# A new order for all steps of an attention and feed-forward kernel, with one pool of single PSUM banks and five output row buffers

## The chip, the cores and the metric

The kernel runs on one core of a Trainium2 chip. The metric is the device time of one execution in microseconds; of several runs the median counts. The engines are TensorE (PE, with its weight loads as PEld), VectorE (DVE), ScalarE (ACT), GpSimd (POOL) and SyncE (SP). Each works through its own queue in order and waits for the others by semaphores.

## The reference, cut to what matters

Batch 8, 8 heads, 576 positions, head size 64. A Nystroem attention with 32 landmarks is followed by a multiplicative feed-forward without a nonlinearity.

```python
q_lm = q.reshape(B, H, 32, 18, D).mean(axis=3)      # the same for k_lm
A  = softmax(q    @ k_lm.T / 8)
Bm = softmax(q_lm @ k_lm.T / 8)
C  = softmax(q_lm @ k.T    / 8)
Z  = Bm.T / (norm_1(Bm) * norm_inf(Bm) + 1e-6)
for _ in range(6):
    Z = 2 * Z - Z @ Bm @ Z
x = heads_side_by_side(A @ Z @ C @ v)                # 4608 x 512
a, b = x @ w1, x @ w2                                # 512 x 1024 each
out = ((a * b) @ w3) @ w_out                         # 1024 x 1024, 1024 x 512
```

## The kernel before

Every piece of work is a Python generator, one for each word of a long text, `ORDER`. A word such as `U3.5` names a step (`U`), a part (3) and a batch (5); each time the word stands in the text, its generator is driven to its next `yield`. A part between two yields is mostly the instructions of one engine. As each engine runs its instructions in the order of issue, the text alone fixes the order on all queues, those of the loads too.

The words:

- `L`, `LO`, `P`: loads of rows of w3 and of w_out (on SP's queue); `LK`, `LQ`: pieces of k and q, `LW`: w1 and w2 (on POOL's); `LV`, `FV`: v (SP's). `GT` is a small POOL copy out of a loaded tile: what stands behind it on POOL is issued once that tile has landed.
- `K` is one warm-up matmul; seven more are written ahead of the order. `KC` makes constants on DVE: masks, unit matrices, the right half of `bt`.
- `S` splits a row block of w_out into two float16 parts (ACT, then DVE); `T` transposes a block of w3 on TensorE and splits it likewise (ACT, DVE); `F` multiplies the two into `w34`, eight parts of three matmuls and a copy on ACT. `T0.1` is the first half of block 1.
- For each batch: `TK`, `TQ` transpose k and q on DVE; `SK`, `SQ` add up the landmarks (DVE for batch 0, else POOL); `E` exchanges quarters (TensorE and ACT for batches 0 and 1, else ACT alone).
- `B`, `N`, `R`, `I0` to `I5`: the scores of the landmarks, their norms, and the six inverse steps. They run for chains of batches: (0), (1, 2), (3, 4), (5, 6, 7).
- `C`, `A`: the two large score blocks with their exponentials on ACT; `V`: C @ v; `M`: the row sums of A and their inverse; `Z`: Z @ C @ v, `G`: its product with w1 and w2.
- `U0` to `U7` (L453 to L460): for one eighth of the hidden width, a product for w1, an ACT copy to `a_sb`, a product for w2, and DVE's multiplication into `ab`. `W` (L495 to L505): for one block of 128 rows of the output, eight products of `ab` with `w34`, an ACT copy into `o_sb`, and two stores on SP.

PSUM has eight banks: three tiles `big` of two banks, one bank `small` (for B, N, R, Z and one F) and one bank `acc` (for F and W). `o_sb` has three buffers.

Of the kernel before, what the change touches and what calls it, by code (L numbers as in the profile page):

```python
# [37 lines left out]
KC SK1.0 F.3 F.3 T0.4 T1.5 F.3 TK0.1 FV.0 F.3 GT.4 T0.4 LW.1 TK1.1 L.6 E.0 F.3 F.3 E.0 B.0 T1.5 B.0
C.0 GT.5 F.3 B.0 F.3 C.0 N.0 T0.5 KC T1.4 TQ1.1 N.0 LW.0 F.3 T1.4 T1.4 SK0.1 C.0 TQ0.1 F.4 LV2.1 F.4
T0.5 F.4 A.0 T0.5 R.0 R.0 R.0 F.4 F.4 F.4 LQ0.2 A.0 I0.0 I0.0 T0.6 LV0.1 SK1.1 L.7 I0.0 A.0 T0.6 C.0  # L40
F.4 I1.0 M0.0 LQ1.3 I1.0 F.4 I1.0 I2.0 T0.6 KC SQ0.1 LW.0 F.4 T1.6 M0.0 F.5 F.5 I2.0 GT.6 I2.0 SQ1.1
M0.0 M1.0 C.0 TK1.2 F.5 V.0 V.0 TQ1.2 M1.0 T1.6 I3.0 F.5 F.5 TK0.2 I3.0 F.5 M1.0 I3.0 LK0.3 F.5 T0.7
F.5 T1.6 V.0 I4.0 V.0 F.5 T0.7 LV1.3 I4.0 F.6 F.6 E.1 F.6 TQ0.2 I4.0 I5.0 E.1 F.6 F.6 I5.0 T1.7 Z.0
SK0.2 Z.0 F.6 T0.7 A.1 Z.0 A.1 T1.7 F.6 F.6 TQ1.3 LQ0.3 A.1 SK1.2 LV3.1 LW.1 LK0.4 G2.0 G0.0 F.6 F.7
T1.7 F.7 G0.0 M0.0 C.1 TQ0.3 LK1.3 SQ0.2 M1.0 G2.0 F.7 C.1 F.7 F.7 C.1 F.7 F.7 C.1 C.1 LQ0.4 G3.0
SQ1.2 G1.0 E.2 E.2 LV1.1 F.7 U0.0 G3.0 B.1 U0.0 G1.0 V.1 U0.0 U4.0 B.1 V.1 TK0.3 U4.0 B.1 V.1 U0.0
U1.0 U4.0 N.1 TK1.3 V.1 LQ1.4 U5.0 U1.0 U4.0 N.1 U5.0 U5.0 U1.0 U2.0 U5.0 U2.0 SK0.3 U1.0 R.1 U3.0
R.1 R.1 U2.0 U3.0 LQ0.5 I0.1 U3.0 LK0.5 SK1.3 U2.0 I0.1 I0.1 U7.0 U3.0 I1.1 F.7 U7.0 I1.1 TK0.4 I1.1
U6.0 W.0 LV0.2 M1.1 U6.0 U6.0 M1.1 U6.0 U7.0 I2.1 U7.0 M0.1 M1.1 M0.1 W.0 I2.1 I2.1 A.2 LV2.2 LK1.5
LK1.4 W.0 I3.1 I3.1 W.1 A.2 I3.1 I4.1 M1.1 M0.1 I4.1 A.2 W.1 I4.1 W.1 I5.1 TQ0.4 I5.1 C.2 Z.1 C.2  # L50
Z.1 I5.1 M0.1 W.2 C.2 Z.1 G0.1 TQ1.4 TK1.4 G1.1 W.2 G0.1 W.0 G1.1 U0.1 U2.1 LV1.2 C.2 U0.1 U0.1 U1.1
W.2 U1.1 SQ0.3 SQ1.3 C.2 W.3 G2.1 SQ0.4 LV3.2 U0.1 U2.1 G3.1 G2.1 V.2 V.2 V.2 U2.1 G3.1 V.2 U1.1
U2.1 SQ1.4 U1.1 U3.1 LQ1.5 U3.1 W.3 TQ0.5 U3.1 SK0.4 U4.1 E.3 SK1.4 LV1.4 U3.1 Z.2 W.3 M0.2 U4.1 Z.2
U7.1 M0.2 U7.1 M0.2 LV2.4 LK1.6 U4.1 E.3 E.4 TK0.5 U5.1 U4.1 U7.1 LV3.3 W.2 LQ0.6 U6.1 U7.1 LV2.3
U5.1 LV3.4 U6.1 Z.2 W.4 E.4 TQ1.5 M1.2 M1.2 U5.1 U6.1 TK1.5 U5.1 B.3 G2.2 M1.2 U6.1 G1.2 G2.2 G0.2
G1.2 W.4 M0.2 G0.2 A.3 M1.2 W.4 G3.2 A.3 A.3 G3.2 LQ1.6 B.3 SK0.5 W.3 W.1 W.5 U3.2 U3.2 C.3 B.3
LQ1.7 C.3 W.5 N.3 LK0.6 W.4 SK1.5 U2.2 LV0.3 LQ0.7 U0.2 C.3 U0.2 N.3 LK1.7 C.3 R.3 U3.2 W.5 U3.2
U0.2 U2.2 U0.2 W.6 SQ0.5 U2.2 U4.2 U2.2 R.3 SQ1.5 U4.2 C.3 W.6 M0.3 M0.3 U1.2 U1.2 W.6 U4.2 U6.2
# [646 lines left out]
```

## Time and profile before

| what | value |
|---|---|
| median of three runs | 261.73 us (260.65 to 262.62) |
| span of the profiled execution, first to last instruction | 260.5 us |
| what lies around that span | not listed; the median is 1.2 us above it, the fastest run 0.15 |
| TensorE busy | 249.7 us, 96% |
| DVE, ACT, POOL busy | 161.5, 159.2, 119.3 us |
| DMA | 37.37 MB, mean 143 GB/s |
| HBM read, written | 38.80 MB, 9.44 MB |

In the rows of the profile the columns are: line, engine, operation, output tile and inputs, shapes, count; then busy time in us and mean ns of one instruction; then the engine's idle time just before them and what ended it. In a timeline a row begins with the start and the length in us. "issue" is a wait for nothing that the profile shows. In a table of windows a row has the stretch, its length, then busy us and count for PE, PEld, DVE, ACT and POOL, the clock granted, DMA's busy share and GB/s. Queue 8 in the DMA table carries instructions: packets, MB, share. In the chain of waits a row is start, length, what.

### The profile page before, as it was taken

Reading aid. Unit: us, or ns where it says so; the run is one execution under the profiler, and the core shown is the slowest. Engines: PE = TensorE matmul, PEld = TensorE weight load, DVE = VectorE, ACT = ScalarE, POOL = GpSimd, SP = SyncE. Lnnn points to the kernel's source line nnn. Section 1 sums busy time; section 2 is a strip of 40 time slices with the busy share of each in tenths; the row PEclk is TensorE's granted clock in tenths of the full one; section 3 lists DMA queues with packets and bytes.
Section 4 is the critical chain, followed back from the end, with each engine's and each line's share of the span. In section 5 each row is a group of like instructions: output and inputs, shape, how many; then the busy total and the mean of one; then the engine's idle time right before and its main releaser. Section 6 shows DMA issues by size and latency. Waiting matters only on the chain.

```text
span 260.5 us, 10306 instructions
## 1 busy us (share of the span) xinstructions
PE 249.7 (96%) x4480; PEld 147.9 (57%) x4480; DVE 161.5 (62%) x306; ACT 159.2 (61%) x349; POOL 119.3 (46%) x199
## 2 busy tenths in 40 slices
PE   6999999989999999899999999999999999999993
PEld 2555554544476558546654764667666465756642
DVE  1579986526687787677658766466474643464510
ACT  3553363525656875995458899847764856456431
POOL 8060697989359989999079796000000000000000
PEclk9999999999999999999999999999999999999999
DMA  6999999999828827999346293130057231621355
GB/s 235 277 305 289 256 257 245 203 169 211 129 72 124 157 63 136 215 250 244 52 111 137 62 258 97 43 87 3 6 126 159 65 81 43 142 65 40 84 115 127
DMA packets 23357, 37.37 MB, mean 143 GB/s; under 512 B 2832, under 2 KB 11536, under 8 KB 23312
## 3 DMA queue, kind: packets, MB, share of 16 engines
q1 hardware_dynamic: 12928, 24.26, 35.6%
q0 software_dynamic: 9792, 11.54, 27.2%
q10 hardware_dynamic: 592, 0.92, 1.0%
q8 instruction: 35, 0.57, 0.9%
q14 instruction: 10, 0.08, 0.1%
HBM read 38.80 MB, written 9.44 MB: 185 GB/s over the span
## 4 chain that ended last, share of the span: by engine, by line
PE 82%; DVE 7%; ACT 5%; DMA 2%; issue 2%; SPq 0%; DVEq 0%; ACTq 0%
PE big L453 21%; PE acc L495 20%; PE acc L537 13%; PE big L438 5%; PE big L347 4%; PE big L389 4%; PE big L523 3%; PE small L537 2%; ACT a_sb L458 2%; DVE ab L460 2%; PE big L366 2%; PE big L495 1%; DMA wof<-in_moe_w_out_dram 1%; PE small L415 1%; PE big L326 1%
## 5 line engine op out<-in xcount | busy, mean ns | idle before, releaser
L453 PE MATMUL big<-ahat,gt 128*128 128x288 f16 x512 | 74.3, 286 | 1.3 <-ACT a_sb L458 0.7
L460 DVE TENSOR_TENSOR ab<-a_sb,big 128x576 f16<-128x576 f16 x64 | 47.1, 750 | 35.3 <-PE big L453 33.5
L495 PE MATMUL acc<-w,ab 128*128 128x512 f16 x264 | 66.7, 380 | 0.0
L453 PEld LDWEIGHTS <-gt 128*128 128x128 f16 x512 | 48.5, 98 | 22.0 <-issue 3.0
L458 ACT CAST a_sb<-big 128x576 f16<-128x576 f32 x64 | 40.2, 639 | 33.2 <-PE big L453 18.8
L194 POOL TENSOR_TENSOR tr<-qkT 128x256 f32<-128x256 f16 x56 | 37.3, 697 | 18.2 <-DVE qkT L165 16.3
L537 PE MATMUL acc<-wsp,w3t 128*128 128x512 f16 x168 | 41.6, 384 | 0.0
L495 PEld LDWEIGHTS <-ab 128*128 128x128 f16 x280 | 25.4, 98 | 27.0 <-issue 4.8
L537 PEld LDWEIGHTS <-w3t 128*128 128x128 f16 x192 | 18.4, 100 | 19.8 <-issue 3.1
L501 ACT ACTIVATE o_sb<-acc 128x512 f32<-128x512 f32 x33 | 19.8, 599 | 10.8 <-PE acc L495 9.5
L445 DVE TENSOR_SCALAR gt<-big 128x1024 f16<-128x1024 f32 x16 | 19.4, 1220 | 7.9 <-PE big L438 7.9
L165 DVE STREAM_TRANSPOSE qkT<-qkn 128x576 uint32<-128x576 uint32 x32 | 24.0, 762 | 0.0
L200 POOL TENSOR_TENSOR tr<-tr 128x256 f32<-128x256 f32 x28 | 19.8, 727 | 0.1
L443 ACT ACTIVATE gt<-big 128x1024 f16<-128x1024 f32 x16 | 15.7, 1024 | 3.4 <-PE big L438 3.3
L438 PE MATMUL big<-wup,zt 64*32 64x512 f16 x512 | 17.3, 379 | 0.3 <-ACT en L370 0.2
L347 PE MATMUL big<-vt,ent 64*32 64x64 f32 x1152 | 14.8, 225 | 0.1
L128 POOL DMA_DIRECT2D qkn<-in_k_dram x16 | 11.5, 722 | 6.9 <-DVE qkT L165 6.9
L347 PEld LDWEIGHTS big<-vt,ent 64*32 64x32 f32 x1152 | 12.7, 105 | 3.4 <-issue 2.3
L284 DVE STREAM_TRANSPOSE ent<-en 128x576 f32<-128x576 f32 x16 | 12.0, 762 | 3.3 <-ACT en L280 3.3
L375 DVE TENSOR_TENSOR ahat<-eat,en 128x576 f16<-128x576 f16 x16 | 13.8, 870 | 0.0
L280 ACT ACTIVATE en<-big 128x288 f32<-128x288 f32 x32 | 12.8, 415 | 0.5 <-PE big L269 0.5
L527 ACT ACTIVATE w3t<-big 128x512 f16<-128x512 f32 (+1 forms) x17 | 9.6, 571 | 5.6 <-PE big L523 5.3
(184 smaller groups left out, 302.8 us busy)
## 6 DMA issues: line engine op xcount, KB each, us to landing
out_dram<-o_sb SPq DMA_DIRECT2D x70, 128.0 KB, 2.4
qkn<-in_q_dram POOLq DMA_DIRECT2D x16, 288.0 KB, 8.5
qkn<-in_k_dram POOLq DMA_DIRECT2D x16, 288.0 KB, 8.9
vt<-in_v_dram SPq DMA_DIRECT2D x16, 288.0 KB, 4.8
...
```

Source lines behind the costliest of these rows:

```text
L165: nc.vector.transpose(out=st["qkT"][:, t, prs].rearrange("p c r q e -> p (c r q e)").bitcast(U32), in_=st["qkn"][:, t, prs, :].rearrange(" ...
L194: add(out=tr[:, c], in0=x[:, c, 0:4, :], in1=x[:, c, 4:8, :], op=ALU.add)
L200: add(out=tr[:, c, 0:2, :], in0=tr[:, c, 0:2, :], in1=tr[:, c, 2:4, :], op=ALU.add)
L347: nc.tensor.matmul(psV[32 * o:32 * o + 32, qd, 0:64], ent[sl, pr, r, :], vt[sl, pr, 64 * r:64 * r + 64], start=(r == 0), stop=(r == RT - 1 ...
L438: nc.tensor.matmul(psG[o:o + 32, qd, :], zt[rs, i, h, :], wup[rs, h, w, fs], start=(i == 0), stop=(i == 1), tile_position=(64 * qd, o))
L445: nc.vector.tensor_scalar(out=g[:, :, w, fs], in0=psG, scalar1=1.0 / ZS, scalar2=None, op0=ALU.mult)
L453: nc.tensor.matmul(p[:, c, 0:HS], st["g"][:, qd, w, 128 * j:128 * j + 128], st["ahat", qd][:, c, :], start=(qd == 0), stop=(qd == 1))
L458: nc.scalar.copy(out=a_sb, in_=p[:, :, 0:HS])
L460: nc.vector.tensor_tensor(out=st["ab"][:, j, st["t0"]:st["t0"] + S].rearrange("p (c s) -> p c s", c=2), in0=a_sb, in1=p[:, :, 0:HS], op=AL ...
L495: nc.tensor.matmul(pso[:, :], ab[:, j, t0:t0 + 128], w34[:, j, :], start=(j == 0), stop=(j == 7))
L501: nc.scalar.activation(out=o_sb, in_=pso, func=AXF.Copy, scale=1.0 / (X64 * X64))
L537: nc.tensor.matmul(psW, w3ts[j, c // 4][:, a, c % 4, :], wsp[:, b, c, :], start=(c == 0 and a + b == 0), stop=(c == 7 and a == 1))
```

## The change

1. `ORDER` is another text: 1,077 words for 1,065. The loads of the start, written ahead of the order until now, become words (`H.0` to `H.4`, `LO.0` to `LO.5`), and so does the load of ACT's table with its first use (`AT`).
2. `small` and `acc` become one pool `one` of two single banks.
3. `o_sb` moves to the pool that holds `ab` and has five buffers in place of three.
4. The unit matrix `eye` goes; its place is the first block of `bt`'s right half. In `R`, the order of the two results is turned round: `sz_` is made first, and `tz_` by one addition from it, in place of two, four or six operations out of PSUM.

```diff
 ORDER = """
-T0.0 S.0 S.0 T0.0 T0.0 T0.0 T0.1 S.2 S.2 LQ0.0 T0.1 K LQ1.0 S.1 T0.1 L.2 LO.6 S.3 F.0 K F.1 S.1
-LK0.0 T0.0 KC F.0 LK1.0 T0.0 T1.0 F.0 T1.0 S.3 S.4 K T1.0 S.5 S.4 F.1 K FV.0 F.1 F.0 T1.1 T1.1 K S.6
-F.0 S.5 T1.1 KC LO.7 KC F.1 F.1 T1.2 F.1 TQ1.0 T1.2 GT.0 LK1.1 L.3 T0.2 LK0.1 S.7 F.0 S.6 F.1 TQ0.0
...
+LO.0 H.3 K K AT LO.3 H.0 S.0 H.1 T0.0 K KC LO.1 H.4 T0.0 K LO.2 S.0 T0.0 H.2 K T0.1 S.1 L.3 LO.4
+T0.0 GT.0 F.0 LO.7 T0.1 LO.6 T1.1 T0.0 S.1 F.0 T0.1 LO.5 T1.0 S.2 T0.0 L.2 LK0.0 F.1 T1.1 S.2 F.0 KC
+S.3 T1.0 T1.1 LK1.0 LQ0.0 S.4 S.7 T1.0 T0.3 F.1 LQ1.0 S.3 S.4 S.5 F.1 F.0 T0.3 LQ0.1 S.5 P.4 KC T1.3
+S.7 F.0 S.6 F.1 T1.2 F.1 LK0.1 T1.3 S.6 F.0 TK0.0 T0.3 LK1.1 F.0 F.1 KC F.1 P.4 T1.3 GT.2 F.0 T0.2
+F.0 TK1.0 T0.2 FV.0 F.1 F.3 F.3 F.3 T0.2 F.1 F.3 F.3 SK0.0 L.5 SK1.0 F.3 F.2 TQ1.0 T0.4 T1.2 T0.4
+F.3 T1.2 TQ0.0 F.3 SQ0.0 F.2 F.2 GT.3 F.2 F.2 SQ1.0 T0.5 GT.4 F.2 F.3 F.2 T0.4 LQ0.2 T0.5 E.0 E.0
+TK0.1 F.2 L.6 KC T1.4 T1.5 F.2 T1.4 B.0 LQ1.1 B.0 F.4 T0.5 T1.5 F.4 GT.5 TK1.1 B.0 N.0 T1.4 F.4 N.0
+C.0 C.0 R.0 LK0.2 R.0 F.4 C.0 T1.5 F.4 R.0 SK0.1 F.5 TQ1.1 I0.0 C.0 A.0 I0.0 I0.0 F.4 A.0 A.0 I1.0
...
+LV2.6 U7.3 U0.3 M0.4 U7.3 Z.4 U3.3 U3.3 W.12 U3.3 E.7 U7.3 W.11 M0.4 U6.3 U6.3 W.12 E.7 W.1 Z.4 U3.3
...
+W.29 U0.7 W.27 W.23 U3.7 U7.7 U0.7 U3.7 U3.7 U3.7 U7.7 W.27 W.29 W.32 U7.7 W.33 W.31 W.33 W.35 W.27
+W.29 W.32 W.27 W.19 W.31 W.33 W.30 W.33 W.34 W.35 W.35 W.34 W.32 W.32 W.31 W.35 W.31 W.34 W.35 W.34
+W.35
 """
...
-    def small():
-        return psp.tile([128, 512], FP32, name="small", bufs=1)
-
-    def acc():
-        return psp.tile([128, 512], FP32, name="acc", bufs=1)
+    def one():
+        return psp.tile([128, 512], FP32, name="one", bufs=2)
...
     def squares(ch):
-        psR = small()
+        psR = one()
...
         yield
-        tz_ = ch["tz"] = pz.tile([128, 6, 32], FP32, name="tz_", bufs=2)
-        for i in range(2 * n):
-            nc.vector.scalar_tensor_tensor(out=tz_[:, i], in0=psR[:, 64 * i:64 * i + 32],
-                                           scalar=ch["nrn"][:, i:i + 1], in1=eye2, op0=ALU.mult, op1=ALU.add)
-        yield
         sz_ = ch["sz"] = pz.tile([128, 6, 64], FP32, name="sz_", bufs=2)
         nc.vector.tensor_tensor(out=sz_[:, x], in0=psR[:, 0:128 * n].rearrange("p (x m) -> p x m", m=64),
                                 in1=ch["nrn"][:, x].unsqueeze(2).to_broadcast([128, 2 * n, 64]), op=ALU.mult)
+        yield
+        tz_ = ch["tz"] = pz.tile([128, 6, 32], FP32, name="tz_", bufs=2)
+        nc.vector.tensor_tensor(out=tz_[:, x], in0=sz_[:, x, 0:32],
+                                in1=eye2.unsqueeze(1).to_broadcast([128, 2 * n, 32]), op=ALU.add)
...
-        pso = big()[:, 0, :] if n > 30 and n % 2 else acc()
+        pso = big()[:, 0, :] if n > 30 and n % 2 else one()
...
-        o_sb = po.tile([128, DM], FP32, name="o_sb")
+        o_sb = pab[0].tile([128, DM], FP32, name="o_sb", bufs=5)
...
-    load_w3(0, slice(0, 256))
-    load_wout(0, nc.scalar)
-    load_w3(0, slice(256, 512))
-    load_wout(1, nc.sync)
-    load_w3(1, 0, nc.scalar)
-    load_wout(2, nc.sync)
...
+    def lead(n):
+        eng = nc.scalar if n == 3 else nc.sync
+        load_w3(n // 3, (slice(0, 256), slice(256, 512), slice(512, 1024), slice(0, 512), slice(512, 1024))[n], eng)
...
-            for qd in range(2):
-                nc.vector.tensor_copy(out=eye[sl, qd, :], in_=ident[sl, sl])
-            yield
-        nc.vector.tensor_tensor(out=eye2, in0=eye[:, 0], in1=eye[:, 0], op=ALU.add)
-        for i in range(6):
-            nc.vector.tensor_copy(out=bt[:, i, 32:64], in_=eye[:, 0])
+            nc.vector.tensor_copy(out=bt[sl, 0, 32:64], in_=ident[sl, sl])
+            yield
+        nc.vector.tensor_tensor(out=eye2, in0=bt[:, 0, 32:64], in1=bt[:, 0, 32:64], op=ALU.add)
+        for i in range(1, 6):
+            nc.vector.tensor_copy(out=bt[:, i, 32:64], in_=bt[:, 0, 32:64])
```

More of the change, by code (lines that the diff above doesn't have):

```diff
@@ L38 @@
[L38 to L58, printed above, removed]
@@ new lines @@
+C.0 C.0 R.0 LK0.2 R.0 F.4 C.0 T1.5 F.4 R.0 SK0.1 F.5 TQ1.1 I0.0 C.0 A.0 I0.0 I0.0 F.4 A.0 A.0 I1.0
+LK1.2 C.0 F.4 LW.1 TQ0.2 TK0.2 SK1.1 F.5 M1.0 T0.6 T0.6 TQ0.1 F.5 F.4 I1.0 LQ1.2 SQ0.1 I1.0 M1.0 L.7
+T1.6 F.5 T0.6 T1.6 T1.6 I2.0 I2.0 FV.0 F.4 TK1.2 M0.0 F.5 F.6 I2.0 I3.0 T1.7 I3.0 F.5 F.5 I3.0 M0.0
+F.6 M0.0 V.0 LW.0 V.0 GT.6 I4.0 F.6 KC LV3.1 F.5 T1.7 I4.0 T1.7 SQ1.1 I4.0 T0.7 E.1 V.0 T0.7 F.5 F.6
+T0.7 V.0 F.6 E.1 LV2.2 I5.0 I5.0 A.1 A.1 LW.0 F.6 SK0.2 F.6 LV0.1 LW.1 A.1 Z.0 TQ1.2 M1.0 SK1.2 Z.0
@@ new lines @@
+M0.0 M1.1 Z.0 C.1 LK0.3 F.6 C.1 LK1.3 F.7 F.7 M1.0 G2.0 LQ0.3 C.1 G0.0 G2.0 C.1 F.7 M1.1 F.7 U4.0
+G0.0 G1.0 LQ1.3 SQ0.2 C.1 U4.0 G3.0 F.6 SQ1.2 M1.1 U0.0 U0.0 G3.0 F.7 LV1.1 G1.0 F.7 TK0.3 U4.0 E.2
+F.7 TK1.3 F.7 U5.0 LQ0.4 U4.0 E.2 LV2.1 B.1 TQ0.3 U0.0 U5.0 B.1 F.7 SK0.3 V.1 V.1 U0.0 U5.0 U2.0 B.1
+U5.0 N.1 R.1 U1.0 U2.0 LK1.4 U2.0 N.1 R.1 U1.0 LK0.4 V.1 U1.0 R.1 U2.0 V.1 U1.0 U6.0 TQ1.3 U3.0 I0.1
+U6.0 I0.1 U3.0 U6.0 I0.1 U3.0 U7.0 SK1.3 U6.0 LQ1.4 U3.0 SQ0.3 U7.0 I1.1 U7.0 I1.1 SQ1.3 I1.1 U7.0
@@ new lines @@
+U4.1 SQ0.4 U5.1 U5.1 U4.1 U4.1 U5.1 SQ1.4 U6.1 U7.1 E.4 U4.1 U6.1 G3.2 SQ0.5 G2.2 E.4 U7.1 LK0.6
+TK0.5 B.3 LQ1.7 LV2.3 G0.2 G3.2 M0.2 U6.1 LV1.3 G2.2 U6.1 G0.2 LQ1.6 B.3 U7.1 U7.1 W.4 A.3 G1.2 A.3
+B.3 W.4 A.3 W.4 U1.2 G1.2 N.3 U1.2 C.3 N.3 R.3 C.3 SQ1.5 LV0.3 R.3 C.3 R.3 LK1.6 U0.2 U0.2 C.3 W.6
+M1.3 U1.2 C.3 W.7 I0.3 M1.3 LK0.7 TQ0.6 I0.3 U1.2 V.3 I0.3 SK0.5 V.3 W.7 LQ0.7 SK1.5 M0.3 M1.3 U0.2
+W.6 M0.3 U6.2 U0.2 TK0.6 I1.3 W.6 V.3 LV0.4 I1.3 U6.2 TQ1.6 U3.2 LK1.7 I1.3 TK1.6 U6.2 V.3 LV2.5 W.5
@@ L230, in scores_b @@
     def scores_b(ch):
-        psB = small()
+        psB = one()
         n = ch["n"]
@@ L473, in down @@
                 c = slice(256 * half, 256 * half + 256)
-                pso = acc() if half else big()[:, 0, :]
+                pso = one() if half else big()[:, 0, :]
                 for j in range(8):
@@ L533, in product @@
     def product(j):
-        psW = small() if j == 1 else acc()
+        psW = one()
         for c in range(8):
```

99 lines of the change are left out of this document (47 added, 52 removed).

## The prediction

> **What bounds the kernel now.** I read the page first (busy time, chain of waits), then the groups of TensorE's instructions by line, then the timeline of the stretches where a row names idle time.
>
> ```profile
> span 260.5 us, 10306 instructions
> PE 249.7 (96%) x4480; PEld 147.9 (57%) x4480; DVE 161.5 (62%) x306; ACT 159.2 (61%) x349; POOL 119.3 (46%) x199
> DMA  6999999999828827999346293130057231621355
> q8 instruction: 35, 0.57, 0.9%
> PE 82%; DVE 7%; ACT 5%; DMA 2%; issue 2%; SPq 0%; DVEq 0%; ACTq 0%
> ```
> ```profile
> L453 PE MATMUL big<-ahat,gt 128*128 128x288 f16 x512 | 74.3, 286 | 1.3 <-ACT a_sb L458 0.7 <-ACT en L280 0.4 <-DVE ab L460 0.2
> L495 PE MATMUL acc<-w,ab 128*128 128x512 f16 x264 | 66.7, 380 | 0.0
> L537 PE MATMUL acc<-wsp,w3t 128*128 128x512 f16 x168 | 41.6, 384 | 0.0
> L523 PE MATMUL big<-ident,w3f 128*128 128x128 f32 x64 | 10.5, 296 | 2.1 <-DVE w3t L529 1.2 <-issue 0.9
> ```
>
> TensorE is busy for 249.7 of 260.5 us and is 82% of the chain. The change leaves its 4480 matmuls as they are (12 warm-ups, the same steps), so the time can only fall by TensorE's idle stretches, by a slow stretch at the start, and by the tail. The two costliest groups, L453 and L495, waited 1.3 and 0.0 us: most of the 11 us outside busy time is start, end and a few single waits. So I go by places. Of the order's 1,077 words (1,065 before; the twelve new ones are loads and the table load, which the code issued ahead of the order) I follow those that touch a place where TensorE waited or may wait, and compare the crowd on each engine by counting words.
>
> **The start, what the new order does there.** In the old order the seven warm-ups run first, then T0.0's first two transposes; its next two wait for DVE to read the same tile, behind S.0's DVE part.
>
> ```profile
> 1.19 3.17 PE L593 MATMUL big<-warm 128*128 128x512 f16 x7 [1.19 <-DVE warm L589]
> 4.16 0.66 PE L523 MATMUL big<-ident,w3f 128*128 128x128 f32 x2
> 4.89 0.69 DVE L512 SCALAR_TENSOR_TENSOR wsp<-wof,wsp 128x512 f16<-128x512 f32 x1 [3.76 <-ACT wsp L510]
> 5.97 1.54 PE L523 MATMUL big<-ident,w3f 128*128 128x128 f32 x6 [1.15 <-DVE w3t L529]
> 7.73 1.49 PE L537 MATMUL acc<-wsp,w3t 128*128 128x512 f16 x3
> 10.63 0.81 PE L537 MATMUL acc<-wsp,w3t 128*128 128x512 f16 x3
> ```
> Three matmuls of 512 columns take 1.49 us at 7.73 and 0.81 at 10.63: up to about 10.5 us the array runs at half its later rate (0.43 us a matmul, then 0.22), and the idle 1.15 us ends 4.7 us before. The new order writes two K ahead of T0.0 and three more ahead of T0.1, and puts T0.1's transposes between the halves of T0.0. All 12 warm-ups are then out by the order's 21st word, and the wait is covered: 1.19 + 9 x 0.43 = 5.05; T0.0 0.5; three K 1.3; T0.1 1.0; T0.0 0.5 gives F.0's first product at about 8.35 us, with no gap before. The run without a gap then begins at 1.19 instead of 5.97, and 4.7 us of it end near 6. The old order reaches the same point (F.0 and F.1 one part each, 12 K) at 10.63 plus its three remaining K, 0.65, so 11.28; the new one at 8.35 + 1.3 = 9.65. Gain 1.6 us. If the rate doubles at 10.5 whatever the gaps do, the new one is there at 10.95: gain 0.3. If it doubles near 6, two us at half rate fall away before 8.35 too: gain 2.8. I take 1.6, the row's own 4.7 us with one us kept back.
>
> [...]
>
> **The loads behind the start.** L.3, LO.4 to LO.7 and L.2 are put in another order on SP's queue; GT.0 now stands ahead of batch 0's k and q pieces on POOL, so these wait for wof[4].
>
> ```profile
> 0.00:5.00 5.00, 3.63 (x9) 1.16 (x9) 0.38 (x2) 2.26 (x4) 4.20 (x18) 1.00 0.53 190
> 5.00:11.00 6.00, 5.03 (x16) 2.68 (x17) 3.75 (x13) 2.67 (x6) 1.11 (x2) 1.00 1.08 297
> 11.00:20.00 9.00, 9.00 (x52) 5.17 (x50) 6.31 (x17) 4.68 (x8) 3.93 (x8) 1.00 1.12 300
> 3.11 1.57 POOL L128 DMA_DIRECT2D qkn<-in_q_dram  x2
> 4.68 1.43 POOL L128 DMA_DIRECT2D qkn<-in_k_dram  x2
> 22.83 0.77 DVE L165 STREAM_TRANSPOSE qkT<-qkn 128x576 uint32<-128x576 uint32 x1
> L194 DVE TENSOR_TENSOR tr<-qkT 128x1024 f32<-128x1024 f16 x2 | 2.4, 1217 | 0.0
> L200 DVE TENSOR_TENSOR tr<-tr 128x512 f32<-128x512 f32 x2 | 1.4, 680 | 0.0
> L205 DVE TENSOR_TENSOR lm<-tr 128x128 f16<-128x128 f32 x4 | 1.0, 289 | 0.1
> 31.67 0.38 PE L212 MATMUL big<-lm,pick 128*128 128x256 f16 x2
> ```
> The last column is GB/s. Up to wof[4] 2.8 MB stand in the queues: 0.95 MB in the first 5 us, the rest at 297 GB/s, so it lands near 12.2, and the four pieces start 9 us later than before (3.11). Beside them 1.28 MB of weights and 0.29 MB of LQ0.1 are under way: 2.7 MB at 300 GB/s put the last piece, LQ1.0, at 21 to 23 us. After it DVE has TQ1.0, T1.2 and TQ0.0 (0.76, 0.64, 0.76 by rows below), SQ0.0 (1.22) and SQ1.0 (five additions from 0.68 down to 0.29, some 2.1): 5.5 us, so 28.5. E.0's matmuls (L212) ran at 31.67; the new order has 1.9 us more TensorE work ahead of them and starts 1.6 earlier, so they are due at 32. Price nothing, with 3.5 us of cover; the upper bound is in the third rival.
>
> **A block's instructions.**
>
> ```profile
> 50.00:53.40 3.40, 2.45 (x13) 0.92 (x10) 0.65 (x2) 0.27 (x1) 3.38 (x6) 1.00 1.23 194
> 53.37 0.66 PE L523 MATMUL big<-ident,w3f 128*128 128x128 f32 x4 [0.95 <-issue]
> ```
> 8960 TensorE instructions in 35 packets of queue 8 are 256 each. The 0.95 us before 53.37 is the one long wait in mid-kernel that names no engine, and DMA's share is 1.23 around it: I read it as a block that came late behind queued loads. Counted in words and priced by the same rows, 256 instructions in that stretch cover 5.2 to 5.5 us of TensorE work in the new order, 4.6 in the old one. A block as late as this one (5.55) still costs 0.1 to 0.35; I take a gain of 0.7. The shortest block under loads stays at 3.9 us in both orders, so a whole such wait may come back: lower bound 0, upper 0.95.
>
> [...]
>
> **DVE's constants and the small operations.**
>
> ```profile
> 35.48 2.29 DVE L617 COPY bt<-eye 128x32 f32<-128x32 f32 x6
> 39.66 0.53 PE L326 MATMUL big<-qkT,lm 32*32 32x288 f16 x32 [1.17 <-DVE w3t L529]
> L165 DVE STREAM_TRANSPOSE qkT<-qkn 128x576 uint32<-128x576 uint32 x32 | 24.0, 762 | 0.0
> L529 DVE SCALAR_TENSOR_TENSOR w3t<-big,w3t 128x512 f16<-128x512 f32 (+1 forms) x17 | 10.9, 644 | 3.3 <-ACT w3t L527 3.3
> L615 DVE TENSOR_TENSOR eye<-eye 128x32 f32<-128x32 f32 x1 | 0.4, 388 | 0.0
> L255 DVE TENSOR_TENSOR bm<-small,rbs 128x128 f32<-128x128 f32 (+2 forms) x4 | 1.2, 292 | 0.3
> L311 DVE SCALAR_TENSOR_TENSOR tz__3643<-small,nrn,eye 128x32 f32<-128x32 f32 x6 | 1.0, 242 | 0.0
> ```
> Six copies of 0.38 us push a w3t part late, and A.0 (L326) waits 1.17 us for its bank. In the new order A.0 follows C.0, R.0 and I0.0, and T1.5's DVE part, the last on DVE to read a bank that A.0 may take, stands eight words ahead: I let that wait go whole (bounds 0 and 1.17). But between E.0's and N.0's first words DVE gets five words instead of two: TK0.1 and TK1.1 (0.76 each), the constants' fifth part (0.39 + 5 x 0.38 = 2.3), T0.5 (0.64), B.0 (some 0.8 by L255 and its neighbours), 5.2 us beside 3.3 us of TensorE work (three F, two T, B.0). The late one is then N.0: I take 0.8 of the 1.9 us excess, since DVE may be ahead at E.0; bounds 0 and 1.9. The 16 L311 (0.24 each) become four additions that read sz_, priced by L255 at 0.29: 2.7 us less on DVE, and four copies and one of bt fewer. TensorE's products of the following inverse wait only where the words stand close, so this is hidden: nothing.
>
> **ACT's crowd.**
>
> ```profile
> 100.00:110.00 10.00, 9.34 (x96) 6.58 (x93) 7.99 (x14) 8.37 (x18) 9.76 (x17) 1.00 1.02 208
> 108.26 1.19 PE L453 MATMUL big<-ahat,gt 128*128 128x288 f16 x8 [0.66 <-ACT a_sb L458]
> 110.32 1.49 PE L438 MATMUL big<-wup,zt 64*32 64x512 f16 x48 [0.24 <-ACT en L370]
> ```
> ACT is busy 8.37 of 10 us here and TensorE waits 0.66, 0.24 and, with L453's row above, 0.4 for L280. From E.3's first word to C.3's first the old order has 21 words for ACT on 21 for TensorE; the new one has 29 on 40. Of these 1.3 us I take 0.9; bounds 0 and 1.3.
>
> **Banks, row buffers, tail.**
>
> ```profile
> L501 ACT ACTIVATE o_sb<-acc 128x512 f32<-128x512 f32 x33 | 19.8, 599 | 10.8 <-PE acc L495 9.5 <-PE big L453 1.1
> 246.39 0.86 PE acc L495 x4
> 256.51 0.42 DVE o_sb L484
> ```
> Two common banks let a down step begin while the one before it is still read (0.60 us, L501); the old order hid that (L495 waited 0.0), so nothing. The same with five row buffers: L501 waited for TensorE, not for an output, and the new order needs the buffers, as it issues W.19's and W.22's outputs only near the end. The tail stays DVE's 0.42 us after the last product, then the store; SP's queue now has W.32, W.31 and W.34 close before W.35's last row, W.34 half a row product (0.86) before the end: +0.2, bounds 0 and 0.6.
>
> **The sum**, against the execution's own span: -1.6 -0.7 -1.17 +0.8 -0.9 +0.2 = -3.4. A new order makes some single waits of its own; the old one has about 0.5 us outside the places named, and I give the new one 0.3 more: -3.1, 257.4. The median of the runs, 261.73, lies 1.2 above that span (their lowest, 260.65, lies 0.15 above): **258.7**. With the bounds' distances added as squares (1.2, 0.25, 0.8, 0.4, 0.2 down; 1.3, 0.7, 1.17, 1.1, 0.9, 0.4 up) its own range is 257.1 to 261.1.
>
> **Rivals.**
> 1. The waits only move: 260.7. The old order was free of waits where its costs were right, and the new one will miss elsewhere; then the start's lower 0.3 remains and the block's 0.7, 1.0 in all. For it: all other waits are under 0.7 us. Against it: both crowds above are thinner in the words. Chance 0.25.
> 2. The 0.95 us has another cause and stays: 258.7 + 0.7 = 259.4. For it: no row names a fetch. [...] Against it: "issue", DMA's share. Chance 0.08.
> 3. Slower: E.0 waits for the late pieces. In the old trace TK1.0, which reads the last issued piece, runs at 22.83, so the four took up to 19.7 us from 3.11. As slow again from 12.2 they end at 31.9, DVE's 5.5 us make it 37.4, E.0 is 5.4 late, and N.0 one more behind batch 1's transposes: 258.7 + 6.4 = 265.1. Each us past 26.5 costs one; it is slower than before from about 29.5. Against it: half the weights run beside them. Chance 0.20.
> 4. The forecast: 0.47, at 258.7.
>
> **Chances.** About 1% is what a measurement tells from no change. Under 259.1 lie most of the forecast (0.33), part of case 2 (0.03) and of case 1 (0.04): 0.40. Over 264.35 lies three quarters of case 3: 0.15. The rest is 0.45. The range, 256.5 to 263.6, leaves out 0.07 below and 0.13 above.
>
> **What would show it.** Right: no idle row before the second L523 at the start, three L537 at 0.81 us from about 8.5; no "issue" row over 0.5 us on TensorE; L326 without a wait, L290 with one under 2; L212 near 32. Wrong: L537 at 1.49 past 10 us (start), a wait of L212 for DVE or for qkn (case 3), idle rows for ACT or DVE that add up to 3 us past 40 (case 1).

## The result, and the profile after

| | before | after |
|---|---|---|
| median, first comparison | 261.81 us | 259.84 us; ratio 0.9927, 95% interval 0.9905 to 0.9949 |
| median, second comparison | 261.80 us | 259.54 us; ratio 0.9904, interval 0.9884 to 0.9923 |
| span of the first profile | 260.5 us | 257.9 us |
| last product of TensorE to the span's end | 4.1 us | 4.7 us |
| TensorE's pauses of over 0.1 us behind its first matmul, added up | 5.24 us | 4.46 us |

The change makes the kernel 0.7 to 1.0% faster, about 2 us; 258.7 was predicted. In every run listed since, the time is the span plus 1.78 us. So the first profile of before, at 260.5, was an execution of some 262.3 us, half a us above the median, and what the text on record took for "around the span" (1.2) was 1.78.

The page of after, top and chain:

```profile
span 257.9 us, 10302 instructions
PE 247.5 (96%) x4480; PEld 148.1 (57%) x4480; DVE 160.1 (62%) x289; ACT 158.1 (61%) x349; POOL 117.2 (45%) x199
PE 81%; DVE 7%; DMA 4%; ACT 3%; issue 2%; DVEq 0%; ACTq 0%
```

As many products, 2.2 us less busy time: by the start below, that is work at half rate that is gone. In the chain, "issue" has kept its 2%, but its waits lie elsewhere now. The groups of TensorE by line, with the idle time before them in the last columns:

```profile
L450 PE MATMUL big<-ahat,gt 128*128 128x288 f16 x512 | 74.6, 286 | 0.2 <-DVE ab L458 0.2
...
L435 PE MATMUL big<-wup,zt 64*32 64x512 f16 x512 | 18.1, 379 | 0.2 <-ACT a_sb L455 0.2
L521 PE MATMUL big<-ident,w3f 128*128 128x128 f32 x64 | 10.0, 279 | 1.2 <-DVE w3t L527 1.0 <-DMA w3f<-in_moe_w_dram 0.2
```

The waits for ACT (1.3 us on L453 and L438 before) are down to 0.2. A.0 no longer waits 1.17 us for DVE, but T1.5's transposes at L521 wait 1.0. One wait named "issue" (0.95 us) has become three (2.8 us). The start on TensorE:

```profile
1.19 4.02 PE L590 MATMUL big<-warm 128*128 128x512 f16 x9 [1.19 <-DVE warm L586]
5.00 0.63 PE L521 MATMUL big<-ident,w3f 128*128 128x128 f32 x2
5.43 1.07 PE L590 MATMUL big<-warm 128*128 128x512 f16 x3
6.34 0.82 PE L521 MATMUL big<-ident,w3f 128*128 128x128 f32 x6
6.99 0.81 PE L535 MATMUL one<-wsp,w3t 128*128 128x512 f16 x3
```

No pause up to here, and the first product triple takes 0.81 us at 6.99, where the first profile of before had 1.49 at 7.73. Then the three issue waits, and the load that POOL had queued just ahead of the first:

```profile
50.32 0.64 POOL L156 DMA_DIRECT2D wup<-in_moe_w_dram  x1
57.56 0.51 PE L323 MATMUL big<-qkT,lm 32*32 32x288 f16 x30 [1.13 <-issue]
97.83 0.59 PE L344 MATMUL big<-vt,ent 64*32 64x64 f32 x37 [0.96 <-issue]
119.60 0.30 PE L363 MATMUL big<-eat,ones 128*128 128x288 f16 x1 [0.71 <-issue]
```

The place where DVE had been expected to be late:

```profile
30.91 0.38 PE L210 MATMUL big<-lm,pick 128*128 128x256 f16 x2
33.37 0.66 PE L521 MATMUL big<-ident,w3f 128*128 128x128 f32 x4 [0.99 <-DVE w3t L527]
35.79 0.41 PE L288 MATMUL one<-bm,mask 128*128 128x64 f32 x2
```

E.0 (L210) starts at 30.91 without a wait, N.0 (L288) has none, and T1.5's transposes wait 0.99 us. And the end, with the queues of SP and ACT:

```profile
250.95 3.75 SPq L503 DMA_DIRECT2D out_dram<-o_sb  x6
...
253.26 0.43 DVE L482 TENSOR_SCALAR o_sb<-one 128x256 f32<-128x256 f32 x1 [8.47 <-DMA out_dram<-o_sb]
253.72 0.47 ACTq L488 DMA_DIRECT2D out_dram<-o_sb  x1
254.79 0.56 SPq L488 DMA_DIRECT2D out_dram<-o_sb  x1
```

DVE has written W.35's last half at 253.69; ACT sends its part at 253.72, SP its own only at 254.79, behind six stores of 0.6 us each.

### The profile page after: what moved, and what is told of

It reads as the page before. It is cut to its first block, busy times and chain, and to the rows that moved or that the text cites. A ratio compares the mean times of both kernels' runs of the same rounds, so it can differ in the third digit from the quotient of the medians.

```text
span 257.9 us, 10302 instructions
## 1 busy us (share of the span) xinstructions
PE 247.5 (96%) x4480; PEld 148.1 (57%) x4480; DVE 160.1 (62%) x289; ACT 158.1 (61%) x349; POOL 117.2 (45%) x199
## 4 chain that ended last, share of the span: by engine, by line
PE 81%; DVE 7%; DMA 4%; ACT 3%; issue 2%; DVEq 0%; ACTq 0%
PE big L450 22%; PE one L493 22%; PE one L535 12%; PE big L435 6%; PE big L344 5%; PE big L386 4%; DMA w3f<-in_moe_w_dram 2%; PE big L521 2%; PE big L363 2%; DMA wof<-in_moe_w_out_dram 1%; PE big L493 1%; PE big L323 1%; PE big L267 1%; PE one L412 1%; ACT a_sb L455 1%
## 5 line engine op out<-in xcount | busy, mean ns | idle before, releaser
L450 PE MATMUL big<-ahat,gt 128*128 128x288 f16 x512 | 74.6, 286 | 0.2 <-DVE ab L458 0.2
L493 PE MATMUL one<-w,ab 128*128 128x512 f16 x264 | 67.3, 380 | 0.0
L450 PEld LDWEIGHTS <-gt 128*128 128x128 f16 x512 | 48.2, 98 | 21.7 <-issue 2.0
L535 PE MATMUL one<-wsp,w3t 128*128 128x512 f16 x192 | 45.8, 379 | 0.0
L192 POOL TENSOR_TENSOR tr<-qkT 128x256 f32<-128x256 f16 x56 | 36.7, 685 | 12.0 <-DVE qkT L163 9.0
L499 ACT ACTIVATE o_sb<-one 128x512 f32<-128x512 f32 x33 | 19.9, 602 | 9.6 <-PE one L493 7.6
L435 PE MATMUL big<-wup,zt 64*32 64x512 f16 x512 | 18.1, 379 | 0.2 <-ACT a_sb L455 0.2
L344 PE MATMUL big<-vt,ent 64*32 64x64 f32 x1152 | 15.9, 224 | 1.1 <-issue 1.0
L344 PEld LDWEIGHTS big<-vt,ent 64*32 64x32 f32 x1152 | 13.3, 105 | 5.3 <-issue 3.2
L525 ACT ACTIVATE w3t<-big 128x512 f16<-128x512 f32 (+1 forms) x17 | 9.5, 567 | 10.8 <-PE big L521 6.5
L527 DVE SCALAR_TENSOR_TENSOR w3t<-big,w3t 128x512 f16<-128x512 f32 (+1 forms) x17 | 10.9, 649 | 4.9 <-ACT w3t L525 4.8
L367 ACT ACTIVATE en<-big 128x576 f32<-128x576 f32 x16 | 10.4, 654 | 4.9 <-PE big L363 4.6
```

The lines of the kernel that those rows point to most:

```text
L192: add(out=tr[:, c], in0=x[:, c, 0:4, :], in1=x[:, c, 4:8, :], op=ALU.add)
L344: nc.tensor.matmul(psV[32 * o:32 * o + 32, qd, 0:64], ent[sl, pr, r, :], vt[sl, pr, 64 * r:64 * r + 64], start=(r == 0), stop=(r == RT - 1 ...
L435: nc.tensor.matmul(psG[o:o + 32, qd, :], zt[rs, i, h, :], wup[rs, h, w, fs], start=(i == 0), stop=(i == 1), tile_position=(64 * qd, o))
L450: nc.tensor.matmul(p[:, c, 0:HS], st["g"][:, qd, w, 128 * j:128 * j + 128], st["ahat", qd][:, c, :], start=(qd == 0), stop=(qd == 1))
L493: nc.tensor.matmul(pso[:, :], ab[:, j, t0:t0 + 128], w34[:, j, :], start=(j == 0), stop=(j == 7))
L499: nc.scalar.activation(out=o_sb, in_=pso, func=AXF.Copy, scale=1.0 / (X64 * X64))
```

## Experiments on the start

Theory 1: the whole gain is at the start, by the K words that cover the pause. Rival: the later order pays.

**The five K of before, moved alone.** The other four leave their places in the rest of this line and in the next one.

```diff
-T0.0 S.0 S.0 T0.0 T0.0 T0.0 T0.1 S.2 S.2 LQ0.0 T0.1 K LQ1.0
+K K T0.0 K K K S.0 S.0 T0.0 T0.0 T0.0 T0.1 S.2 S.2 LQ0.0 T0.1 LQ1.0
...
```

> The kernel before, with nothing changed but the places of its five K: two ahead of T0.0, three right behind its first part. Theory 1 (the whole gain of the change is at the start: the array is at full rate some 5 us earlier and the gap of 1.15 us is covered, 2.4 + 1.0 less the five warm-ups that now run slow, 5 x 0.21 = 1.0): 1.5 to 2.5 us faster than before, products of L537 at 0.81 us from about 8, all later waits as before (0.95 at the third block, 1.17 at A.0). Rival (the gain comes from the later order, from DVE and from the banks): within 0.3 us of before.

Measured: 261.96 us, ratio to before 1.0014 (0.9999 to 1.003). No gain, so theory 1 falls in this form. The array was at full rate from 4.7 us on (two transposes took 0.38 us at 4.67, where the first profile of before has 0.66 at 4.16; three K took 0.81 at 4.89), and yet the next products did not come earlier (timeline of this run):

```profile
6.73 0.81 PE L537 MATMUL acc<-wsp,w3t 128*128 128x512 f16 x3
8.61 0.60 PE L537 MATMUL small<-wsp,w3t 128*128 128x512 f16 x2 [1.06 <-ACT w3t L527]
```

**Before once more, unchanged.**

> The kernel before once more, unchanged, for a second profile. Theory 5 (the first profile, span 260.5 us, was one of its longest executions: what lies around the span was 1.78 us in every run listed since, so it took 262.3 us): a span of 258.8 to 260.2, and the full rate of the array somewhat earlier than the 10.5 us of the first profile, which the step on the start took as given. Rival (the first profile was typical): L537 at 1.49 us until 10.5 again.

Measured: 261.76 us, ratio 0.9997 (0.998 to 1.0014), the profiled execution with a span of 259.7. Its start, TensorE and ACT:

```profile
6.04 0.88 PE L523 MATMUL big<-ident,w3f 128*128 128x128 f32 x6 [1.33 <-DVE w3t L529]
8.70 0.61 PE L537 MATMUL small<-wsp,w3t 128*128 128x512 f16 x2 [0.70 <-ACT w3t L527]
7.53 0.63 ACT L510 ACTIVATE wsp<-wof 128x512 f16<-128x512 f32 x1 [2.33 <-DMA wof<-in_moe_w_out_dram]
```

Full rate at 6.04 already (six transposes in 0.88 us), where the first profile had half rate until 10.5 (1.54 us for the six at 5.97, 1.49 for three products at 7.73), with the same matmuls ahead and a like pause (1.33 and 1.15 us). The last product came only 0.89 us earlier for it (255.53 against 256.42): ACT stands 2.33 us waiting for a row block of w_out, and what is ready earlier on TensorE waits for ACT. So in this execution the loads set the start of the old order, and the array's rate hides behind them. The windows of 5 to 8 and 8 to 11 us, first this run, then after (last columns: DMA's share and GB/s):

```profile
5.00:8.00 3.00, 1.96 (x11) 1.10 (x11) 0.99 (x2) 0.67 (x2) 1.12 (x2) 1.00 1.06 329
8.00:11.00 3.00, 2.06 (x11) 0.98 (x11) 2.81 (x11) 1.96 (x5) 0.00 (x0) 1.00 1.11 259
```
```profile
5.00:8.00 3.00, 3.00 (x19) 2.14 (x18) 2.00 (x4) 1.85 (x4) 0.00 (x0) 1.00 1.11 395
8.00:11.00 3.00, 2.83 (x18) 1.56 (x17) 2.87 (x9) 2.23 (x4) 0.00 (x0) 1.00 0.96 360
```

In after, the four pieces of q and k are issued from 11.8 us on, behind GT.0, and until then the weights have the queues to themselves: 395 and 360 GB/s for 329 and 259. Of the 1.77 MB that before's second profile moves from 5 to 11 us, 0.38 are pieces of q and k on POOL's queue; weights are 1.39 MB there and 2.26 in after.

**After, with its five K put back behind the first products, and T0.1 behind T0.0's second transposes.**

```diff
-LO.0 H.3 K K AT LO.3 H.0 S.0 H.1 T0.0 K KC LO.1 H.4 T0.0 K LO.2 S.0 T0.0 H.2 K T0.1 S.1 L.3 LO.4
-T0.0 GT.0 F.0 LO.7 T0.1 LO.6 T1.1 T0.0 S.1 F.0 T0.1 LO.5 T1.0 S.2 T0.0 L.2 LK0.0 F.1 T1.1 S.2 F.0 KC
+LO.0 H.3 AT LO.3 H.0 S.0 H.1 T0.0 KC LO.1 H.4 T0.0 LO.2 S.0 T0.0 H.2 S.1 L.3 LO.4
+T0.0 T0.1 GT.0 F.0 LO.7 T0.1 LO.6 T1.1 T0.0 S.1 F.0 K K T0.1 LO.5 T1.0 S.2 T0.0 L.2 LK0.0 F.1 K K T1.1 S.2 F.0 K KC
...
```

> The kernel after, with its five K and T0.1's transposes put back to where the old order had them (behind the first products). Theory 1: the gap ahead of T0.0's second transposes comes back, the first products take 1.49 us again, and the time is 1.0 to 2.5 us longer than after, within 0.5 us of the median of before. Rival (the later order pays): at most 0.3 us longer than after.

Measured: 260.96 us, ratio 0.9977 (0.9957 to 0.9998), 1.1 to 1.4 us longer than the two medians of after. The pause of 1.17 us was back, and so was the half rate until past 10 us: three products took 1.49 us at 7.38. The rate of the loads stayed. The windows of 5 to 8 and 8 to 11 us, first the run with the K moved on the old loads, then this one:

```profile
5.00:8.00 3.00, 2.22 (x13) 0.99 (x10) 0.96 (x2) 0.95 (x3) 1.12 (x2) 1.00 1.05 327
8.00:11.00 3.00, 2.16 (x11) 1.07 (x12) 2.90 (x11) 1.86 (x5) 0.00 (x0) 1.00 1.13 269
```
```profile
5.00:8.00 3.00, 1.95 (x8) 1.58 (x9) 1.68 (x3) 1.30 (x3) 0.00 (x0) 1.00 1.01 377
8.00:11.00 3.00, 2.87 (x12) 1.31 (x10) 2.19 (x7) 1.97 (x5) 0.00 (x0) 1.00 0.94 356
```

The rate of the loads goes with their order and not with the K. So in the new order, where the loads come in time, the places of K and T0.1 are worth 1.1 to 1.4 of the 2 us; on the old loads the K moved alone are worth nothing. That is the net worth: in this run's trace the start costs more, 2.4 us at the wait near 57 (60.00 against 57.56), of which 1.1 are left at the one near 119 (120.69 against 119.60), as the issue waits on the way are shorter (0.82 and 0.43 us for 1.13, 0.96 and 0.71). The remaining 0.6 to 0.9 us are the loads' new order and everything later together; no run separated these two. The second profiles of both kernels (the one of after follows below) point at the start: the marked pauses of TensorE up to 10 us are 2.27 us in before and 0.17 in after, all later ones 3.42 and 3.28; TensorE is busy for 248.1 and 248.4 us.

## Experiments on blocks of instructions

Theory 2: a packet of 256 TensorE instructions is asked for when the block before it begins, and stands behind data already queued. As the moment of asking I take TensorE's instruction 256 n + 192, the count that fits the places of the waits: with its semaphore and drain instructions counted, from 0, the issue waits of the first profiles stand ahead of instruction 962 in before and of 1217, 3010 and 4034 in after, one or two past it. The traces show when a packet comes; the asking is my estimate.

**Loads on POOL moved, first try.**

```diff
-V.0 LW.0 V.0 GT.6 I4.0 F.6 KC LV3.1 F.5 T1.7 I4.0 T1.7 SQ1.1 I4.0
+V.0 V.0 GT.6 I4.0 F.6 KC LV3.1 F.5 T1.7 I4.0 T1.7 SQ1.1 LW.0 I4.0
...
-SK0.4 W.1 M1.1 C.2 LV1.2 LQ1.5 M0.1 I4.1 I4.1 C.2 LQ0.5 C.2 W.1
+SK0.4 W.1 M1.1 C.2 LV1.2 M0.1 I4.1 I4.1 C.2 C.2 W.1
...
-Z.1 SK1.4 W.2
+Z.1 SK1.4 LQ1.5 LQ0.5 W.2
```

> The kernel after, with three words of loads on POOL put later: the first LW.0 behind SQ1.1, LQ1.5 and LQ0.5 behind SK1.4. TensorE's words are untouched. Theory 2 (a block of 256 instructions is asked for when the one before begins, and its packet stands behind data of loads that are already queued): the issue waits of 1.13 us near 56.4 and 0.95 us near 96.9 go, the packets asked for near 51.3 and 90 come within 1.5 us of the asking, the wait of 0.70 us near 118.9 stays (its block is 2.4 us long): 1.5 to 2.1 us faster than after. Rival (the waits belong to the place in the program, or to something else on PE's queue): both stay, within 0.3 us of after. Second rival: the delay only moves to the next block and costs the same there.

Measured: 260.39 us, ratio 0.9976 (0.9946 to 1.0005), 0.6 to 0.9 us longer than after. The place near 96.9 did as expected: its packet came some 0.3 us after the asking instead of some 4.5 and the wait went, though 0.34 us came up at the next block. The place near 56.4 got worse, because I had taken the wrong LW.0: the one ahead of that block was the second, and now both were issued together, at 49.99 us. The wait, and the windows behind it (the column after POOL's busy time is the granted clock):

```profile
58.46 0.52 PE L323 MATMUL big<-qkT,lm 32*32 32x288 f16 x30 [1.68 <-issue]
```
```profile
58.00:60.00 2.00, 1.54 (x35) 0.77 (x35) 0.53 (x1) 0.95 (x2) 2.00 (x3) 0.92 1.10 241
60.00:62.00 2.00, 2.00 (x9) 1.29 (x7) 0.00 (x0) 0.98 (x3) 2.00 (x4) 0.50 1.06 270
62.00:64.00 2.00, 2.00 (x39) 0.76 (x38) 1.42 (x3) 1.07 (x6) 2.00 (x3) 0.72 1.04 229
```

After the longer pause the clock is 0.50 in one window, 0.92 and 0.72 in its neighbours. If it is either 1.00 or 0.50 at each moment, that is 0.08/0.5 x 2 + 2 + 0.28/0.5 x 2 = 3.44 us at half rate, an estimate, which costs another 1.7 us. Its ten times fall into two groups, seven from 259.5 to 261.0 and three from 262.3 to 262.5. The mean granted clock was 0.992 or 0.993 in these three and 0.99 in the profiled one (260.96), and 0.997 or more in the other six, so the three may have had such a stretch as well.

**The right one, the second LW.0, moved.**

```diff
-A.1 A.1 LW.0 F.6 SK0.2 F.6 LV0.1 LW.1
+A.1 A.1 F.6 SK0.2 LW.0 F.6 LV0.1 LW.1
```

> The kernel after, with one word moved: the second LW.0 (half of w1, on POOL) behind SK0.2 instead of two words ahead of it, so that it is issued some 3 us later. Two loads queued together ahead of that block (the run before this one) lengthened the issue wait near 56.4 from 1.13 to 1.68 us. Theory 2 (the block's packet stands behind queued data): with no load queued when the block is asked for near 51.3, its packet comes within 1.7 us and the wait goes; the ones near 96.9 and 118.9 stay: 0.8 to 1.3 us faster than after. Rival (the wait hangs on the place in the program): it stays at 1.1, within 0.3 us of after.

The DMA queues of after from 51.3 to 55.1 us and from 55.1 to 56.2, then of this run from 52.8 to 54.1 (queue 0 is POOL's, queue 8 the instructions):

```profile
q0 software_dynamic: 289, 0.56, 92.0%
```
```profile
q0 software_dynamic: 53, 0.10, 89.0%
q8 instruction: 1, 0.02, 5.5%
```
```profile
q8 instruction: 1, 0.02, 5.5%
q0 software_dynamic: 1, 0.00, 0.1%
```

In after, the packet asked for at 51.30 came at 55.14, once 289 packets of POOL's load were through. Here it was asked for at 52.03 and came at 52.90, before the load's data, and the wait near 56.4 is gone: theory 2 holds at this place. The time, 259.46 us (0.9914, 0.9881 to 0.9947), is the same as after's. Its profiled execution (260.52) has two new waits for DVE, 1.05 us together; that they gave back the 1.13 us is argued from this one trace:

```profile
72.02 1.20 PE L344 MATMUL big<-vt,ent 64*32 64x64 f32 x84 [0.46 <-DVE ab L458]
99.86 1.39 PE L450 MATMUL big<-ahat,gt 128*128 128x288 f16 x10 [0.59 <-DVE ab L458]
```

**Six loads more on POOL, where there are none.** The word stands behind U1.4's last part.

```diff
+    def extra():
+        st, old = sts[4], sts[6]
+        nc.gpsimd.tensor_copy(out=old["qkn"][:, :, :, 0:1], in_=st["ab"][:, 1, st["t0"]:st["t0"] + 8].rearrange("p (t c x) -> p t c x", t=2, x=1))
+        for t in (0, 1, 0):
+            for c in range(2):
+                qk_piece(old, 6, t, slice(2 * c, 2 * c + 2))
```

> The kernel after, with six loads of 288 KB on POOL added in a stretch that has none (batch 6's k and q once more into their old tile, started by a copy that reads U1.4's result, near 168 us); nothing reads them. Theory 2: the blocks asked for near 169.8 and 174.5, whose packets came 1.2 and 1.4 us after the asking, come 3 to 6 us after it and at least one issue wait of 0.7 to 4 us appears there: 1 to 4 us slower than after. Rival (loads and blocks do not meet; the waits belong to their places): no new wait, within 0.4 us of after.

Measured: 261.05 us, ratio 0.9994 (0.9966 to 1.0022), 1.2 to 1.5 us longer than after; six of ten times from 260.3 to 261.2, four from 262.5 to 262.9. The block asked for at 174.01 came 3.80 us later (1.43 in after), and where after has no wait there is one of 1.25. The queues from 174.0 to 177.7 us, from 177.7 to 178.8, and the wait:

```profile
q0 software_dynamic: 555, 0.60, 95.4%
...
```
```profile
q0 software_dynamic: 200, 0.22, 115.9%
q8 instruction: 1, 0.02, 5.4%
```
```profile
180.11 0.44 PE L386 MATMUL big<-sz__3832,tz__3830 32*32 32x64 f32 x28 [1.25 <-issue]
```

What makes the two groups of times, the one profile (260.69) does not show. The run settles that queued loads make a wait at a place that had none.

**As many bytes on SP's queue.**

```diff
-        for t in (0, 1, 0):
-            for c in range(2):
-                qk_piece(old, 6, t, slice(2 * c, 2 * c + 2))
+        for t in (0, 1, 0):
+            nc.sync.dma_start(out=old["qkn"][:, t].rearrange("p c f -> p (c f)").bitcast(FP32),
+                              in_=q[6].rearrange("h s d -> (h s d)").rearrange("(p f) -> p f", p=128)[:, 0:1152])
```

> The same place as the run with six loads on POOL, but three loads of 590 KB on SP's queue, as many bytes written. Theory 2 in its wide form (any data queued ahead holds the block up): blocks near 169.8 and 174.5 late by 2 to 5 us, a wait of 0.5 to 3 us. Narrow form (only what POOL queues does): packets within 1.5 us of the asking, no new wait, within 0.4 us of after.

Measured: 259.35 us (0.9915, 0.9891 to 0.9939), no longer than after. The block of 169.80 came 3.04 us after the asking (1.18 in after), and a wait of 0.39 us for it appeared at 175.15. The next one came at 176.73, 1.6 us after the end of that wait (1.43 after the asking in after). SP's loads hold a block up too, so the wide form is right, by less than POOL's; whether that is the queue or the shorter time the three loads took, this run does not tell.

**After once more.**

> The kernel after once more, unchanged, for the spread of its times and a second profile of it. Theory (its waits at block crossings depend on where each load's data stand in the queues at that moment): the waits near 56.4, 96.9 and 118.9 differ by some tenths of a us from the first profile, some executions are 1 us and more longer, the median is within 0.6 us of 259.84. Rival (they are fixed): the same waits within 0.1 us, times within 0.4 us of each other.

Measured: 259.54 us (258.81 to 259.94). Its issue waits were 0.76 near 56.7, 0.71 near 86, 0.59 near 119 and none near 96.9: 2.1 at blocks, in part at other places than in the first profile. One profile of such a wait is one draw. T1.5's transposes have no wait in it: TensorE reaches them later, held 0.47 us by a load of w3 at 30.4.

## Experiments on DVE, the tail, and together

**The fifth KC behind T0.5's DVE part.**

```diff
-TK0.1 F.2 L.6 KC T1.4 T1.5 F.2 T1.4 B.0 LQ1.1 B.0 F.4 T0.5 T1.5 F.4 GT.5 TK1.1 B.0 N.0 T1.4 F.4 N.0
+TK0.1 F.2 L.6 T1.4 T1.5 F.2 T1.4 B.0 LQ1.1 B.0 F.4 T0.5 KC T1.5 F.4 GT.5 TK1.1 B.0 N.0 T1.4 F.4 N.0
```

> The kernel after, with one word moved: the fifth KC (five copies into bt, 1.47 us, and one addition) behind T0.5's part on DVE instead of nine words ahead of it. Theory 3 (DVE has more between E.0 and N.0 than TensorE has, and what is late is the bank that T1.5 writes): the wait of 0.99 us at L521 near 32.4 goes, N.0 and A.0 stay without one, 0.7 to 1.0 us faster. Rival: the wait moves on to B.0, N.0 or R.0, and the time is within 0.3 us of after.

Measured: 258.78 us, ratio 0.9896 (0.9858 to 0.9934), 0.8 to 1.1 us below after; the intervals overlap. All eight transposes in one piece:

```profile
33.66 1.04 PE L521 MATMUL big<-ident,w3f 128*128 128x128 f32 x8
```

Nothing behind it waits for DVE in turn: the crowd that the prediction saw was real, and the late one was T1.5's bank. But the trace does not show the gain at this place. Loads of w3 made TensorE wait 1.5 us up to 31 us (0.17 in after), and at the next issue wait this execution is 0.3 us behind after, which has 57.56:

```profile
57.86 0.52 PE L323 MATMUL big<-qkT,lm 32*32 32x288 f16 x30 [0.76 <-issue]
```

It is ahead, by 0.85 us near 119 (118.75 against 119.60), only behind the crossing near 97, where it has no wait and after 0.96. After's second profile has no wait at T1.5 either. So what this word is worth is not settled.

**Two late stores on ACT's queue.**

```diff
-            nc.sync.dma_start(out=rows[b0 + u // RT, u % RT], in_=o_sb[64 * i:64 * i + 64, :])
+            eng = nc.scalar if i and n in (31, 34) else nc.sync
+            eng.dma_start(out=rows[b0 + u // RT, u % RT], in_=o_sb[64 * i:64 * i + 64, :])
```

> The kernel after, with the second stores of W.31 and W.34 on ACT's queue instead of SP's. Theory 4 (SP issues its last stores back to back, some 0.6 us each, and W.35's last one leaves 1.1 us after DVE has written its row): SP's last store is issued near 253.7 instead of 254.8, the span ends 0.6 to 1.1 us earlier. Rival (the end is set by ACT's half of that row, issued at 253.7, or by the landing): within 0.3 us of after.

Measured: 258.16 us, ratio 0.9867 (0.984 to 0.9893), 1.4 to 1.7 us below after. SP's last store now follows DVE at once (below, in the run with KC), and from the last product to the end it is 4.25 us instead of 4.7. That is 0.5 us. The rest, about 1 us, the stores cannot have brought, as they stand at the end: TensorE begins its wait near 118 1.06 us earlier than in the first profile of after, and again the crossing near 97 had no wait. Whether the other four executions owe their time to that, no profile shows. Its profiled execution, 260.96 us, is its longest and shows a second case of the lowered clock:

```profile
119.92 0.30 PE L363 MATMUL big<-eat,ones 128*128 128x288 f16 x1 [2.09 <-issue]
```
```profile
120.00:122.00 2.00, 2.00 (x11) 1.15 (x12) 1.18 (x2) 0.78 (x2) 0.29 (x1) 0.79 0.53 73
122.00:124.00 2.00, 2.00 (x85) 1.28 (x85) 0.75 (x3) 1.27 (x3) 1.29 (x2) 0.50 0.54 87
124.00:126.00 2.00, 2.00 (x46) 1.43 (x33) 1.81 (x5) 0.85 (x2) 0.77 (x2) 0.85 0.15 28
```

By the same estimate, again 0.84 + 2 + 0.6 = 3.44 us at half rate.

**Four edits together:** KC, the second LW.0, the two stores, and LK0.7 with LQ0.7 behind SK1.5.

> The kernel after with four edits together: the fifth KC behind T0.5's part on DVE; the second LW.0 behind SK0.2; LK0.7 and LQ0.7 (needed 20 and 14 us later) behind SK1.5, so that fewer loads are queued when the short block near 115 us is asked for; the second stores of W.31 and W.34 on ACT's queue. If the pieces add (0.99 at T1.5, 1.13 and part of 0.70 at two blocks, 0.9 at the tail): 256.5 to 257.5 us, 2.3 to 3.3 us faster than after. Rival (they do not add: as TensorE comes earlier, the loads of w3 and the blocks are late by as much more): 258 to 258.8.

Measured: 258.56 us, ratio 0.9878 (0.9858 to 0.9898). The rival was right, they do not add. Two waits for DVE in it:

```profile
70.17 1.06 PE L344 MATMUL big<-vt,ent 64*32 64x64 f32 x71 [0.40 <-DVE ab L458]
97.95 0.77 PE L450 MATMUL big<-ahat,gt 128*128 128x288 f16 x5 [0.53 <-DVE ab L458]
```

**KC and the stores alone.**

> The kernel after with two of the four edits of the combined run: the fifth KC behind T0.5's part on DVE, and the second stores of W.31 and W.34 on ACT's queue; all loads on POOL as in after. Theory 6 (the moved loads gave back what they gained, in waits of 0.4 and 0.5 us for ab of DVE near 70 and 97.5 and 0.37 near 85, which the runs with LW.0 later have and the others mostly not): these three are gone, a wait of 0.7 near 56.5 is back, 257.6 to 258.3 us, no longer than the combined run's 258.56. Rival (the loads' move was worth its 0.8 to 1.1 us and something else holds the combined run up): 259 to 259.5.

Measured: 257.97 us (257.36 to 258.82), ratio 0.9859 (0.983 to 0.9887): the fastest version, 1.6 to 1.9 us below after (whose intervals begin at 0.9905 and 0.9884). The waits for DVE and the 0.37 near 85 of the combined run are gone, 1.3 us in all, and one of 0.74 at the block near 56.4 is back; all pauses of over 0.1 us add up to 2.49 us for 2.90, and the median is 0.59 lower. The intervals of these two runs overlap, so it is certain only that moving those loads brought nothing. To the stores alone (258.16) KC adds 0.2 us, within the noise. And of the 2.3 us between the spans of the first profiles of after and of this version (255.6), 0.5 are the tail. The rest comes at the crossings near 57 (a wait of 0.74 for 1.13), 97 (none for 0.96) and 119 (0.32 for 0.71), which neither edit touches; up to the first of them both stand at 56.4. Why DVE is late for `ab` in both runs with LW.0 later was not tried. The tail of this version:

```profile
251.44 0.42 DVE L482 TENSOR_SCALAR o_sb<-one 128x256 f32<-128x256 f32 x1 [8.46 <-DMA out_dram<-o_sb]
251.90 0.47 SPq L488 DMA_DIRECT2D out_dram<-o_sb  x1
```

## Why the prediction was right, and where not

The span came out at 257.9 for 257.4 predicted, the time at 259.84 and 259.54 for 258.7. That it came so close is luck: in the first profiles the start gave about 3 us (2.2 of busy time and 1.0 of pauses up to 20 us) where 1.6 was priced, and the blocks cost 1.85 us where a gain of 0.7 was.

- **Start (-1.6).** The size was near by the medians of the experiment that puts the words back (1.1 to 1.4). The reading was not: of three profiles with the pause, two have half rate until past 10 us (three products in 1.49 us) and one full rate before 6.1 (six transposes in 0.88); what sets that moment, no run shows. And where the loads of w_out bind, the same K bring nothing (261.96 us, ratio 1.0014). The step that failed is "the loads behind the start, price nothing": holding q and k back behind GT.0 was priced as a risk only, while with it 2.26 MB of weights came from 5 to 11 us in place of 1.39, which let the covered start pay. Rival 3, the same loads too late for E.0, did not happen: the four had landed by 23.0 us, its "as slow again" held for none of them.
- **Block (-0.7, bounds 0 and 0.95).** Failed, in sign: 0.95 became 2.8 us (0.60 and 2.1 in the second profiles). Naming the cause was right, and rival 2 is out. The working looked at one block, and at words per block; it did not ask which loads are queued when each of the 35 is asked for, nor see that the block near 118.6 is under 3 us long, where a wait comes even with a packet 1.06 us after the asking. The lower bound should have reached to a loss of some 2 us.
- **bt copies and A.0 (-1.17).** Right: A.0 has no wait. **N.0 (+0.8)** was 0.99 at T1.5 in the first profile: the cause was right, by the KC run, the place wrong, and the size hangs on when TensorE gets there (0.96 in two other runs, none in after's second profile).
- **ACT's crowd (-0.9).** Right, about 1.1: L453's and L438's waits for ACT were 1.3, L450's and L435's are 0.2.
- **Tail (+0.2, bound 0.6).** Mis-sized: +0.6, because six stores of 0.6 us stand ahead of SP's last one, which the count "W.34 half a row product before the end" left out.
- **From span to median (+1.2).** Mis-sized: 1.78 lies around every span, and the first profile of before was half a us above its median.
- **The squares on DVE, the PSUM pool, the row buffers (nothing).** No row names them. The order keeps two products or two `W` open at once (F.1 with F.3, W.7 with W.8), so it needs the one pool; this was not tried apart.
